# Cutting one weight load of a decode block into 8, 8 and 112 partitions, and joining the loads of x

## The chip, the core and the metric

The kernel runs on one core of a Trainium2 chip. The core has five engines with queues of their own: PE (matrix multiply), DVE (vector), ACT (scalar), POOL, and SP, which here only issues transfers. Sixteen DMA engines carry what SP and ACT issue. The metric is the device time of one execution in microseconds (us), lower is better. Three runs of the kernel before gave a median of 659.67 us (659.04 to 659.94).

## What is computed

Two tokens (batch 2, one position each) go through one attention block with a long cache and one gated feed-forward block:

```python
def ref(x, k_cache, v_cache, wq, wo):          # layernorm(x) comes in
    q = (x @ wq).reshape(B, Sq, Hq, Dh).transpose(0, 2, 1, 3)
    scores = einsum("bhqd,bhkd->bhqk", q, k_cache) * Dh ** -0.5
    o = einsum("bhqk,bhkd->bhqd", softmax(scores), v_cache)
    return o.transpose(0, 2, 1, 3).reshape(B, Sq, Hq * Dh) @ wo

h = x + ref(layernorm(x), k_cache, v_cache, wq, wo)
n = layernorm(h)
gate, up = n @ W_gate, n @ W_up
out = h + ((gate * (gate > 0)) * up) @ W_down
```

B is 2, D is 512, there are 32 heads of Dh = 128 and 8192 cached positions; F of the feed-forward block is 1376. Everything is bf16. Keys and values are 2 x 32 x 8192 x 128 x 2 bytes = 134.2 MB each, so the kernel has to read 268.4 MB of cache and some 12.6 MB of weights, for two rows of output.

## The kernel before

**Tiles.** The cache is walked in steps of four heads (`Step`, lines 130 to 157): 15 full steps, and then the last four heads as two half steps of two heads (`p0`, `p1`). A full key or value tile has 128 partitions of 64 KB, 8.4 MB; a half one has half of that. Three buffers `bufs[0]` to `bufs[2]` (printed as `tile`) hold them in turn. For each step DVE multiplies keys by the query (`products`, L375), folds the products by halves (`scores`, L393, L395); PE does part of the tokens by transposing (L349) and multiplying (L340); ACT takes the exponentials; PE multiplies by the values (`values`, L446).

**Loads.** All large loads are issued by SP in the order of the program (`load_tile`, L165): W_q, the first keys and values, then a key or a value tile whenever a buffer comes free. A load that has to wait holds back all that SP issues after it. The order around the end is: keys of `p0` and `p1`, values of `p0`, the first sixteen heads of W_o (`load_set(0)`, L567 and L571), values of `p1`, the rest of W_o (sets of 8, 4 and 2 heads by `load_set`, then heads 30 and 31 by L589 and L590), W_gate and W_up (L612), W_down (L616, L621). `load_set(k)` puts n heads of W_o into 128 partitions so that each partition gets one contiguous row of n x 1024 bytes: 16 KB for the first set.

**x.** The two rows of x go to two partitions of `xr`, which lies in `bufs[2]` beside W_q. ACT issues five loads for them (L189 to L192), of 256, 256, 256, 128 and 128 elements, each to one partition. PE transposes x (L238), DVE normalises it (`ln_cols`), PE multiplies it by W_q (L252), and when the queries are spread (L259, L267) the second key tile may be loaded over W_q.

**Completion semaphores.** The framework gives the loads, in program order and over SP and ACT together, eight completion semaphores in turn. A load that takes a semaphore has to wait, on its queue, until the load that had it eight places before has landed, unless that is known already. There are 56 transfers in the program. So a transfer more or less ahead of a load changes which older load it waits for.

**The end.** `attend_set(0)` (L635, instructions of L502) uses the first sixteen heads of W_o while the last values are still on their way. After the values of `p1` (L469), the rest of W_o (L502, L509), the second layer norm without its scale (L659 to L677), W_gate and W_up (L686) and W_down (L719), two rows are written out (L736).

Of the kernel before, what the change touches and what calls it, by code (L numbers as in the profile page):

```python
# [13 lines left out]
def _free(t, offset, dims):  # L14

    return bass.AP(tensor=t.tensor, offset=t.offset + offset, ap=[t.ap[0]] + [list(d) for d in dims])


def _dram(t, offset, dims):
    return bass.AP(tensor=t.tensor, offset=t.offset + offset, ap=[list(d) for d in dims])  # L20
# [3 lines left out]
def kernel(  # L24
# [13 lines left out]
    nc = tc.nc  # L38
    P = nc.NUM_PARTITIONS
    B, Sq, D = A_x.shape  # L40
    _, Hkv, Sk, Dh = A_k_cache.shape
# [83 lines left out]
    wo = bufs[0][:, HALF:TILE]  # L125
# [60 lines left out]

    with tc.manual_schedule():

        for b, k, n in ((0, 0, 2), (0, 2, 2), (1, 0, 2), (1, 2, 1), (1, 3, 1)):  # L189
            nc.scalar.dma_start(  # L190
                out=xr[b:b + 1, k * P:(k + n) * P], in_=_dram(A_x, b * D + k * P, [[D, 1], [1, n * P]]),
            )  # L192
# [9 lines left out]
            out=nscale, in_=nscale, compare_op=ALU.not_equal, fill=-SCALE,  # L202
# [5 lines left out]
            out=ident_f, in_=ident_f, compare_op=ALU.not_equal, fill=1.0,  # L208
# [4 lines left out]
            out=sel, in_=sel, compare_op=ALU.not_equal, fill=1.0,  # L213
# [9 lines left out]
            out=pick, in_=pick, compare_op=ALU.not_equal, fill=1.0,  # L223
# [24 lines left out]
        for g0 in range(0, NQ, 4):  # L248
            for n0 in range(NH * g0 * Dh, NH * (g0 + 4) * Dh, 4 * Dh):
                q_ps = ps2.tile([B, 4 * Dh], f32, tag="o")  # L250
                for c in range(KC):
                    nc.tensor.matmul(  # L252
                        out=q_ps, lhsT=xn[:, c, :], rhs=wq_sb[:, c, n0:n0 + 4 * Dh], start=(c == 0), stop=(c == KC - 1),
                    )
                nc.vector.tensor_copy(qrow[:, n0:n0 + 4 * Dh], q_ps)
            for b in range(B):
                r_ps = ps2.tile([P, 4, Dh], f32, tag="tp")
                for j in range(NH):
                    nc.tensor.matmul(  # L259
                        out=r_ps[j * (P // NH):(j + 1) * (P // NH)], lhsT=sel[:, b, 0:P // NH],  # L260
# [5 lines left out]
        for j in range(2):  # L266
            nc.tensor.matmul(  # L267
                out=r_ps[j * (P // 2):(j + 1) * (P // 2)], lhsT=sel[:, B - 1, :],
# [31 lines left out]
        def own_sums(i):  # L300
            b, g0, n = groups[i]
            nc.vector.tensor_tensor(
                out=zc[:, b, g0:g0 + n, :], in0=_free(zs, b * NQ + g0, [[1, n], [0, NH]]),
                in1=_free(own, 0, [[0, n], [1, NH]]), op=ALU.mult,
            )
# [65 lines left out]
        def products(s, t0=0, t1=None):  # L371

            n = (s.nv if t1 is None else t1) - t0
            kv = _free(s.kt, t0 * Dh, [[Dh, n], [1, Dh]])
            nc.vector.tensor_tensor(out=kv, in0=kv, in1=_free(s.qr, 0, [[0, n], [1, Dh]]), op=ALU.mult)  # L375
# [186 lines left out]
        place_own(s)  # L562
        products(p0, 0, p0.na)
        own_sums(Q)
        def load_set(k):
            h0, n, at = SETS[k]
            nc.sync.dma_start(  # L567
                out=wo[:, at * D:(at + n) * D], in_=_dram(A_wo, h0 * Dh * D, [[n * D, P], [1, n * D]]),
            )

        load_set(0)  # L571
        products(p0, p0.na)

        at = [0, 0]
# [12 lines left out]
        for k in range(1, len(SETS)):  # L587
            load_set(k)
        nc.sync.dma_start(out=wo[:, HM * D:(HM + 1) * D], in_=_dram(A_wo, HM * Dh * D, [[D, P], [1, D]]))  # L589
        nc.sync.dma_start(  # L590
            out=wo[:, (HM + 1) * D:Hq * D], in_=_dram(A_wo, (HM + 1) * Dh * D, [[P // 4 * D, 4], [D, P // 4], [1, D]]),
# [19 lines left out]
        for w, src in ((0, B_W_gate), (1, B_W_up)):  # L611
            nc.sync.dma_start(  # L612
                out=wgu[:, w].rearrange("p c f -> p (c f)"), in_=_dram(src, 0, [[KC * F, P], [1, KC * F]]),
            )
        for q0 in range(AGAIN, P, AGAIN):
            nc.sync.dma_start(  # L616
                out=wd_sb[q0:q0 + AGAIN, FC - 1, :], in_=_dram(B_W_down, (F - P + q0) * D, [[D, AGAIN], [1, D]]),
            )
        for f0, n in FSETS[:-1]:
# [10 lines left out]
            out=z2_ps, lhsT=ones, rhs=_free(zc, ((B - 1) * NQ + groups[Q][1]) * NH, [[1, nb]]), start=True, stop=True,  # L630
# [63 lines left out]
        for c in range(KC):  # L694
            nc.tensor.transpose(hT_ps[:, c, :], hb[:, c].rearrange("p k b -> p (k b)"), ident)
        nc.scalar.activation(
            out=hrow.rearrange("q (p c) -> q p c", c=KC), in_=hT_ps.rearrange("q c p -> q p c"), func=ACT.Copy,
# [9 lines left out]
            out=gate, in0=g_ps, scalar=0.0, in1=_free(rvar, 0, [[0, FC], [1, B]]), op0=ALU.max, op1=ALU.mult,  # L707
# [59 lines left out]
```

## Time and profile before

| what | value |
|---|---|
| median of three runs | 659.67 us (659.04 to 659.94) |
| the profiled execution: its own time / its span | 659.39 us / 657.5 us |
| bytes moved, mean rate | 281.37 MB, 428 GB/s |
| busy: DVE, PE, ACT, POOL | 85%, 54%, 19%, 4% |
| mean granted PE clock | 0.76 |

The span runs from the first to the last instruction; the execution's own time is 1.9 us longer. A chain of waits is followed back from the last instruction to what released each step. Beside instructions the trace holds one record for each packet that a DMA engine moved: when it began, how long it took, how many bytes it had and the queue that it came from. It does not name the engine. Here a row of one partition is one packet, and each engine ends a load with a packet of 4 bytes. On one engine a packet begins where the one before it ended, so that the packets of an engine can be followed by their times. Such numbers are called packet records below.

### The profile page before, as it was taken

To read this page: it belongs to the slowest core of one execution; us is meant where nothing else is said; L and a number is where in the kernel's file an instruction comes from. 1 tells how busy PE (TensorE), PEld (TensorE's weight loads), DVE (VectorE), ACT (ScalarE), POOL (GpSimd) and SP (SyncE) were. 2 spreads that over 40 slices of the span, in tenths; PEclk is the share of its full clock that TensorE was granted. 3 is DMA by queue.
4 is the path that set the end of the run, shared out by engine and by line. 5 is a ranking of instruction groups with operands and counts; after the bars stand their busy time and mean duration, and the time that the engine had idled before them with its cause. 6 is when DMAs were issued, how large, how long until landed. Compare 5 with 4: busy or idle time off the path is not lost.

```text
span 657.5 us, 5117 instructions
## 1 busy us (share of the span) xinstructions
PE 352.1 (54%) x2118; PEld 158.9 (24%) x2118; DVE 558.1 (85%) x252; ACT 123.6 (19%) x337; POOL 24.1 (4%) x36
## 2 busy tenths in 40 slices
PE   0730934809175380926539092552918458291997
PEld 0310311304022130312204031220403224030456
DVE  0599697988979799897979989796997969999982
ACT  0230030200203020030301103030210304201870
POOL 3080000000000000000000000000000000000020
PEclk9975775958778596877959687695968869686895
DMA  9999999999999999999999999999999999999997
GB/s 383 447 444 447 387 440 443 447 399 444 439 443 436 419 436 435 439 439 436 423 443 424 439 440 427 447 416 443 439 423 440 423 443 436 423 444 413 425 425 291
DMA packets 6948, 281.37 MB, mean 428 GB/s; under 512 B 809, under 2 KB 1422, under 8 KB 1934
## 3 DMA queue, kind: packets, MB, share of 16 engines
q1 hardware_dynamic: 6916, 281.06, 99.1%
q8 instruction: 16, 0.26, 0.1%
q14 instruction: 6, 0.05, 0.0%
q10 hardware_dynamic: 10, 0.00, 0.0%
HBM read 281.05 MB, written 0.00 MB: 427 GB/s over the span
## 4 chain that ended last, share of the span: by engine, by line
DVE 42%; DMA 37%; PE 18%; ACT 1%; issue 1%; ACTq 0%; SPq 0%; DVEq 0%
DMA tile<-in_A_k_cache_dram 30%; DVE tile L375 19%; DVE tile L393 18%; PE pv_ps L446 16%; DMA tile<-in_A_wo_dram 4%; DVE scol L395 2%; DMA tile<-in_A_x_dram 2%; DMA tile<-in_B_W_down_dram 1%; PE q_ps L252 1%; DVE pgq L420 1%; ACT ecol L415 1%; DVE pm L399 1%; DVE qrep L395 0%; DVE pm L410 0%; DVE hmax L412 0%
## 5 line engine op out<-in xcount | busy, mean ns | idle before, releaser
L446 PE MATMUL pv_ps<-tile,pgq 128*16 128x512 bf16 x960 | 244.3, 421 | 235.8 <-DVE pgq L420 223.2
L375 DVE TENSOR_TENSOR tile<-tile,qrep 128x29696 bf16<-128x29696 bf16 (+3 forms) x16 | 232.4, 14524 | 44.9 <-DMA tile<-in_A_k_cache_dram 44.9
L393 DVE TENSOR_TENSOR tile<-tile 128x14848 bf16<-128x14848 bf16 (+7 forms) x68 | 236.4, 3477 | 2.2
L446 PEld LDWEIGHTS <-pgq 128*16 128x16 bf16 x960 | 91.6, 97 | 378.1 <-DVE pgq L420 234.5
L451 ACT ACTIVATE pv<-pv_ps 16x512 f32<-16x512 f32 (+1 forms) x16 | 9.4, 589 | 243.7 <-PE pv_ps L446 243.6
L350 ACT ACTIVATE tile<-t_ps 128x1024 bf16<-128x1024 bf16 x53 | 52.6, 1022 | 12.6 <-PE t_ps L349 12.1
L415 ACT ACTIVATE ecol<-scol,nmax 128x256 bf16<-128x256 f32 x14 | 7.1, 508 | 196.1 <-DVE nmax L414 196.1
L340 PE MATMUL row_ps<-tile,qz 128*24 128x512 bf16 (+1 forms) x98 | 30.1, 389 | 18.0 <-ACT tile L350 17.9
L349 PE MATMUL t_ps<-ident,tile 128*128 128x128 bf16 x424 | 32.3, 229 | 13.0 <-DMA tile<-in_A_k_cache_dram 13.0
L349 PEld LDWEIGHTS <-tile 128*128 128x128 bf16 x424 | 25.8, 103 | 28.1 <-issue 14.2
L395 DVE TENSOR_REDUCE scol<-tile 128x232 f32<-128x1856 bf16 (+1 forms) x14 | 28.9, 2067 | 0.5
L641 POOL TENSOR_TENSOR tile<-ident 6x2 bf16<-6x2 bf16 x1 | 2.1, 2147 | 583.5 <-ACT tile L381 583.5
L420 DVE TENSOR_TENSOR pgq<-ecol,ownb 128x1024 bf16<-128x1024 bf16 x15 | 10.4, 692 | 10.3 <-ACT ecol L415 10.3
L381 ACT ACTIVATE tile<-tile 128x128 bf16<-128x128 bf16 x60 | 17.6, 293 | 1.9 <-DVE tile L375 1.9
L281 POOL COPY qzp<-qTs 128x4 bf16<-128x4 bf16 x1 | 15.0, 14982 | 26.1 <-DVE qTs L276 26.1
L375 DVE TENSOR_TENSOR tile<-tile,qpair 128x4096 bf16<-128x4096 bf16 (+3 forms) x4 | 15.5, 3883 | 0.0
L340 PEld LDWEIGHTS <-qz 128*24 128x24 bf16 (+1 forms) x98 | 7.9, 92 | 27.6 <-issue 22.7
L239 DVE CAST xc<-x_ps 128x8 f32<-128x8 bf16 x1 | 0.2, 167 | 15.5 <-PE x_ps L238 15.5
L367 ACT ACTIVATE scol<-sc_ps 32x24 f32<-32x24 f32 (+1 forms) x56 | 11.7, 209 | 7.7 <-PE sc_ps L362 7.2
L362 PE MATMUL sc_ps<-ident_f,tile 24*128 24x24 f32 (+2 forms) x68 | 7.2, 220 | 11.1 <-ACT tile L358 11.1
L358 ACT ACTIVATE tile<-row_ps 24x512 f32<-24x512 f32 (+2 forms) x17 | 10.0, 586 | 13.5 <-PE row_ps L340 13.5
L381 ACT ACTIVATION_READ_ACCUMULATOR tile<-tile 128x1 f32 x60 | 11.2, 186 | 0.0
(133 smaller groups left out, 143.8 us busy)
## 6 DMA issues: line engine op xcount, KB each, us to landing
tile<-in_A_k_cache_dram SPq DMA_DIRECT2D x2, 4096.0 KB
tile<-in_A_v_cache_dram SPq DMA_DIRECT2D x2, 4096.0 KB, 19.6
tile<-in_A_wq_dram SPq DMA_DIRECT2D x1, 4096.0 KB, 12.2
tile<-in_A_wo_dram SPq DMA_DIRECT2D x1, 2048.0 KB
tile<-in_B_W_gate_dram SPq DMA_DIRECT2D x1, 1376.0 KB, 22.8
tile<-in_B_W_up_dram SPq DMA_DIRECT2D x1, 1376.0 KB
tile<-in_A_wo_dram SPq DMA_DIRECT2D x1, 1024.0 KB, 23.8
tile<-in_B_W_down_dram SPq DMA_DIRECT2D x1, 640.0 KB
```

The source lines that it names most:

```text
L281: nc.gpsimd.tensor_copy(qzp[:, :, 6:8], qTs[:, B - 1, Hq - NH:Hq].rearrange("p (k j) -> p k j", j=2),)
L340: nc.tensor.matmul(out=row_ps, lhsT=z, rhs=s.kt[:, (nv + c0 + k) * Dh:(nv + c0 + k + 4) * Dh], start=(u == 0), stop=(u == U - 1),)
L349: nc.tensor.transpose(t_ps[:, k, :], s.kt[:, t * Dh:(t + 1) * Dh], ident)
L350: nc.scalar.activation(out=s.kt[:, (nv + c0) * Dh:(nv + c0 + TPC) * Dh], in_=t_ps.rearrange("p t s -> p (t s)"), func=ACT.Copy,)
L367: nc.scalar.activation(out=scols[s.i][r, nv:s.nt].rearrange("p (u t) -> p t u", t=4), in_=sc_ps[r, :, :, j], func=ACT.Copy,)
L375: nc.vector.tensor_tensor(out=kv, in0=kv, in1=_free(s.qr, 0, [[0, n], [1, Dh]]), op=ALU.mult)
L381: nc.scalar.activation(out=kv, in_=kv, func=ACT.Copy, accum_out=scols[s.i][:, t:t + 1])
L393: nc.vector.tensor_tensor(out=lo, in0=lo, in1=hi, op=ALU.add)
L395: nc.vector.tensor_reduce(out=scol[:, s.na:s.nv], in_=_free(s.kt, s.na * Dh, [[Dh, s.nv - s.na], [1, 8]]), axis=AXIS.X, op=ALU.add,)
L415: nc.scalar.activation(out=ecol, in_=scols[s.i], func=ACT.Exp, scale=SCALE, bias=nmax, accum_out=zs[:, s.b, s.g:s.g + 1],)
L420: nc.vector.tensor_tensor(out=s.pg, in0=_free(ecol, 0, [[VG, s.nt // VG], [0, NH], [1, VG]]), in1=_free(ownb, 0, [[0, s.nt // VG], [VG, NH ...
L446: nc.tensor.matmul(out=pv_ps[s.i][r, :], lhsT=s.pg[:, u].rearrange("p j t -> p (j t)"), rhs=s.vt[:, u * VG * Dh:(u + 1) * VG * Dh], start= ...
```

## The change

The first sixteen heads of W_o are loaded by three transfers, of partitions 0 to 7, 8 to 15 and 16 to 127, instead of one. The rows and their bytes stay the same, and the three are issued one after another where the one was. x is loaded by three transfers of 512, 256 and 256 elements instead of five. There are again 56 transfers.

```diff
-        for b, k, n in ((0, 0, 2), (0, 2, 2), (1, 0, 2), (1, 2, 1), (1, 3, 1)):
+        for b, k, n in ((0, 0, 4), (1, 0, 2), (1, 2, 2)):
             nc.scalar.dma_start(
                 out=xr[b:b + 1, k * P:(k + n) * P], in_=_dram(A_x, b * D + k * P, [[D, 1], [1, n * P]]),
             )
...
-        def load_set(k):
+        def load_set(k, cuts=(0, P)):
             h0, n, at = SETS[k]
-            nc.sync.dma_start(
-                out=wo[:, at * D:(at + n) * D], in_=_dram(A_wo, h0 * Dh * D, [[n * D, P], [1, n * D]]),
-            )
-
-        load_set(0)
+            for q0, q1 in zip(cuts, cuts[1:]):
+                nc.sync.dma_start(
+                    out=wo[q0:q1, at * D:(at + n) * D],
+                    in_=_dram(A_wo, (h0 * Dh + q0 * n) * D, [[n * D, q1 - q0], [1, n * D]]),
+                )
+
+        load_set(0, (0, 8, 16, P))
```

The other calls, `load_set(1)` to `load_set(3)`, have no cuts and stay one transfer each.

## Prediction

> **What bounds the kernel now.** I read the page's slices and queues first, then stretches of the span, then the chain of waits, then SP's timeline, and last the packet records.
>
> The slices and the queues of the page (packets, MB, share of 16 engines):
>
> ```profile
> DMA  9999999999999999999999999999999999999997
> q1 hardware_dynamic: 6916, 281.06, 99.1%
> q8 instruction: 16, 0.26, 0.1%
> q10 hardware_dynamic: 10, 0.00, 0.0%
> ```
>
> The DMA engines are busy from the first slice to the last but one. The stretches (busy time of PE, PEld, DVE, ACT, POOL; granted clock, DMA share, GB/s) say the same:
>
> ```profile
> 31.00:330.00 299.00, 148.26 (x756) 63.65 (x755) 266.46 (x85) 46.50 (x97) 14.98 (x1) 0.74 1.00 434
> 330.00:600.00 270.00, 147.26 (x738) 63.13 (x738) 241.59 (x88) 43.41 (x87) 0.00 (x0) 0.76 1.00 433
> 620.00:640.00 20.00, 18.50 (x173) 10.12 (x172) 18.50 (x22) 15.52 (x80) 3.66 (x2) 0.99 0.99 422
> ```
>
> The packet records give the rate of one engine: the 3840 packets of 64 KB take 2418 ns each, almost without exception, so 27.1 GB/s, and sixteen times that is 434. Each of the sixteen carries eight rows of every 128-partition load, one after another, in the order of issue. The kernel ends when the slowest of the sixteen has done its share. DVE's 85% is beside it.
>
> The chain of waits (start, us, what):
>
> ```profile
> 2.11 12.96 DMA tile<-in_A_x_dram
> ...
> 30.96 41.50 DMA tile<-in_A_k_cache_dram
> 72.48 15.64 DVE tile L375
> ...
> 618.99 24.67 DMA tile<-in_A_wo_dram
> ...
> 644.18 9.77 DMA tile<-in_B_W_down_dram
> 653.94 0.04 issue
> 653.99 0.60 PE d_ps L719 x15
> 654.58 0.03 issue
> 654.61 0.33 PE d_ps L719 x4
> ```
>
> x heads it and the last W_down load closes it: PE's last four products start when the last rows land. SP's timeline about the loads in question:
>
> ```profile
> 605.16 0.33 SPq L165 DMA_DIRECT2D tile<-in_A_v_cache_dram  x1
> 605.54 0.42 SPq L567 DMA_DIRECT2D tile<-in_A_wo_dram  x1
> 617.67 0.33 SPq L165 DMA_DIRECT2D tile<-in_A_v_cache_dram  x1
> ...
> 624.84 0.33 SPq L612 DMA_DIRECT2D tile<-in_B_W_gate_dram  x1
> 629.68 0.33 SPq L612 DMA_DIRECT2D tile<-in_B_W_up_dram  x1
> 639.34 4.03 SPq L616 DMA_DIRECT2D tile<-in_B_W_down_dram  x3
> ```
>
> SP runs far ahead: W_o's first set is issued at 605.5 and has landed by 629.7, when W_up, which waits for it, goes out.
>
> **Who is slowest.** Following the packets, the engines finish W_up in three groups: six at 647.8 to 648.0, three at 649.3 to 649.6, seven at 650.7 to 650.9. The spread is made by the sixteen instruction packets of queue q8: each holds up one engine by a pause of about 0.95 us and a next packet of 2890 instead of 2418 ns, 1.4 us in all. They go round eight engines in turn (the engine of 37 us again at 440, that of 95 at 500), so eight get two each by the end (seven of them before W_up ends) and eight none; two of the latter get two 8 KB instruction packets instead, some 0.7 us each. The engine that carries x ends in the first group, as far as its packets can be told from others.
>
> **The change, part by part.**
>
> *x.* On its engine each x load is a data and a 4-byte packet, and between any two of these the queue gives way to one W_q packet of 1213 ns: about 2.45 us a load. The 4-byte packets end at 1.9, 7.6, 10.1, 12.5 and 15.0 us. With three loads the last is the third, 10.1: 4.9 us earlier (bounds: 2.45 if the longer rows cost a turn more, 4.9). From x to normalised x takes 3.4 us (15.20 to 18.56), so 13.6, when W_q's last packet (12.9) has landed; the L252 products move from 18.6 to 13.7 and the second key load from 31.0 to 26.1. What hides it: the first values fill the queue until about 51.6 (first keys landed at 32.2, plus 8 x 2.42), and DVE's first products start at 32.41, 0.2 us after those keys. So 0; the cover is 20 us deep. Two packet pairs fewer on one engine are 0.05 us.
>
> *SP's queue.* Two more issues of 0.43 + 0.05 us at 605.5, 1.0 us. Behind them stands the L165 load of 617.67, which waits for PE: hidden under 11 us.
>
> *Completion semaphores.* The total is 56 again, so from the values of `p1` on each load has the same semaphore as before, but the older users differ. Heads 24 to 27 and 28 to 29 now wait for the key halves of `p0` and `p1` (landed before 618: free), head 30 for the values of `p0` (624.8), head 31, W_gate and W_up for the three pieces. Before, head 30 went out at 619.5 and W_gate waited for those values. All SP work behind head 30 is thus held until 624.8 and then follows the pieces. At that moment the values of `p1` (9.7 us) are still queued, so with pieces up to 5 us late the engines don't run dry: 0. `attend_set(0)` runs at 634.6 and has 4.9 us of room.
>
> *The pieces.* A row is a packet, so a load of 8 partitions occupies eight engines at most, one 16 KB packet each, and 112 partitions are seven packets on each of sixteen. A 16 KB packet takes 613 ns (mean of 128). If both small loads go to the same eight engines, these carry nine packets instead of eight, +0.61 us, and the others seven, -0.61 us. The x loads bear out that a small load is not spread: ten packets for five loads. [...]
>
> *Eight streams into eight partitions.* The trace has no such load. Lower end: each engine keeps its pace, 0.61 us a load; upper end: all eight packets go one after another, 4.9 us. Two rows bound it closer. The 32-partition W_down loads (sixteen streams, two partitions a stream) show packets of 46 ns, as 128-partition loads of the same row do, so two partitions a stream are enough: four streams into eight partitions, two turns, 1.2 us. In the large loads sixteen streams share 128 partitions, eight a stream: one stream, 4.9 us. I take the middle of these by ratio, four partitions a stream, four turns of 0.613: 2.45 us a load. The W_down rows, taken alone, would make it 0.61. [...] By the W_down row the time would be 659.1. Packets of 1 KB may be too short to show it.
>
> *Sum.* The lower eight: 2 x 2.45 + 7 x 0.613 = 9.19 us where eight packets took 4.90: +4.3. The 112-partition load is taken at seven packets' time, its nearest row being the 128-partition one; its upper end is four streams a turn in all seven turns, 17.2 us. How much reaches the end depends on who these eight are: if they hold one of the last group, all 4.3; if all end at 648, 4.3 - 3.1 = 1.2. As x's engine is of the first group, I take them to be the eight that get no 16 KB instruction packets; the latest of those end W_up at 649.6, 1.3 us before the last. So +3.0 us. Behind it W_down follows on the same engines, and PE from the values of `p1` (639.3) to W_up (651.3) has only 0.3 us of idle before W_up, so both move with the slowest engine. On the profiled execution 659.39 + 3.0 = 662.4; the median of the runs shown is 0.28 above it, so 662.7.
>
> **The rivals.**
>
> *No sharing, 0.15.* Each engine keeps its pace (the 46 ns rows speak for it; sixteen engines never pass 434 GB/s together, which leaves room for the opposite). Then the nine packets fall on engines with 1.3 us of slack, and the last group, which sets the end, carries one packet less: -0.61 us, 659.1. It decides as soon as a small load costs under about 1.2 us. This one isn't slower.
>
> *Sharing in the 112 rows too, 0.25.* Seven rows an engine no longer lie as in a 128-partition load. If streams meet two at a time, that load takes 8.6 instead of 4.3 us: 4.3 more, 667.0; on all sixteen engines there is no slack for it. Only the regular packets of the 128-partition loads speak against it.
>
> *The two small loads on different eights, 0.05.* Every engine has eight packets again, and the turns fall apart: 659.7, no change.
>
> *x reaches the end, 0.05.* If the 12.96 us of x at the head of the chain were the true bound, 4.9 us would go: 654.8. The DMA share of 1.00 from 31 us on speaks against it.
>
> **How the numbers follow.** The forecast, 0.50, is 662.7, its own range 660.5 to 664.5 (slack 3.1 to none). The range for 8 in 10 reaches from the no-sharing case, 658.8, to 668.0, just above the 112-row case. This kernel's measurement can tell about 0.2% (1.3 us) from no change. Slower: 0.25 and 0.46 of the forecast's 0.50 = 0.71. Within: 0.15, 0.05 and the forecast's low end 0.04 = 0.24. Faster: 0.05.
>
> **What would show it.** Right: x's last completion at 10.1 us, the second key load issued near 26, and no gain from either at 72; 16 KB packets of the small loads longer than 613 ns, about 2.4 us; W_up's issue, which waits for the 112 rows, near 634 instead of 629.7; the last W_down product about 3 us later. Wrong: those packets at 611 ns (then 659.1), or packets of the 112 rows well above 613 ns (then 667 and more), or an instruction packet that falls on another engine, 1.4 us either way.

## The result, and the profile after

| | before | changed |
|---|---|---|
| median of four runs | 659.58 us (659.04 to 659.94) | 667.40 us (666.47 to 668.18) |
| the profiled execution, its own time / its span | 659.39 / 657.5 us | 668.18 / 666.4 us |
| mean rate of the span | 428 GB/s | 422 GB/s |

The changed kernel is slower: ratio 1.0119, 95% interval 1.0104 to 1.0134, or 7.8 us. The forecast was +3.0 us. The time lies near the upper end of the range, at the rival "Sharing in the 112 rows too" (667.0).

The slices and queues of the changed kernel's page (rows and queues as before, with the rate of each slice):

```profile
DMA  9999999999999999999999999999999999999996
GB/s 378 441 438 441 441 438 425 401 441 438 441 433 438 437 430 433 429 429 442 429 441 426 437 438 429 441 434 429 441 430 429 433 438 437 430 414 437 290 369 252
q1 hardware_dynamic: 6932, 281.06, 98.8%
q8 instruction: 16, 0.26, 0.1%
q10 hardware_dynamic: 6, 0.00, 0.0%
```

The busy row shows nothing: every slice but the last is a 9. The rate shows it: one slice (the 38th, 616 to 633 us) has 290 GB/s where its neighbour has 437. The stretches of the changed kernel say so more sharply (columns: busy time of PE, PEld, DVE, ACT, POOL; granted clock, DMA share, GB/s):

```profile
31.00:330.00 299.00, 146.31 (x740) 62.74 (x740) 265.95 (x83) 45.95 (x94) 0.00 (x0) 0.74 1.00 434
330.00:600.00 270.00, 147.23 (x738) 62.97 (x738) 241.72 (x88) 43.41 (x87) 0.00 (x0) 0.75 1.00 433
620.00:640.00 20.00, 15.76 (x111) 7.26 (x110) 17.15 (x14) 14.79 (x77) 3.50 (x2) 1.00 1.01 275
```

Up to 600 us nothing has changed. Between 620 and 640 the DMA engines are as busy as ever (1.01) and move 275 GB/s instead of 422: their packets take longer. In 20 us, 147 GB/s less is 2.9 MB, which at 434 GB/s takes 6.8 us to make good. That is most of the loss in one line.

The chain of waits of the changed kernel (start, us, what):

```profile
1.51 8.62 DMA tile<-in_A_x_dram
...
26.93 45.70 DMA tile<-in_A_k_cache_dram
...
72.75 15.64 DVE tile L375
...
619.28 33.23 DMA tile<-in_A_wo_dram
...
653.02 9.79 DMA tile<-in_B_W_down_dram
662.81 0.04 issue
662.85 0.60 PE d_ps L721 x16
...
663.48 0.33 PE d_ps L721 x4
```

x lands at 10.1 instead of 15.1 us and the second key load goes out 4.0 us earlier; yet the product of these keys begins at 72.75 instead of 72.48. The W_o piece of the chain is one of the loads of the rest of W_o, which queue behind the first set and the values of `p1`; it has grown from 24.67 to 33.23 us, and the last product begins at 663.48 instead of 654.61, 8.9 us later.

SP's timeline of the changed kernel (start, us, line, what is issued):

```profile
605.26 0.33 SPq L165 DMA_DIRECT2D tile<-in_A_v_cache_dram  x1
605.64 1.05 SPq L568 DMA_DIRECT2D tile<-in_A_wo_dram  x3
617.94 0.36 SPq L165 DMA_DIRECT2D tile<-in_A_v_cache_dram  x1
...
630.09 0.33 SPq L614 DMA_DIRECT2D tile<-in_B_W_gate_dram  x1
638.89 0.33 SPq L614 DMA_DIRECT2D tile<-in_B_W_up_dram  x1
648.29 3.92 SPq L618 DMA_DIRECT2D tile<-in_B_W_down_dram  x3
```

W_up, which waits for the 112-partition piece, goes out at 638.89; before, it went at 629.68, and the forecast was about 634. Two places on PE show who waits for the late bytes (PE's timeline, in brackets the idle time before and what ended it; the kernel before first, then the changed one):

```profile
634.56 2.29 PE L502 MATMUL att_ps<-orow,tile 128*128 128x2 bf16 x64
...
639.46 1.84 PE L469 MATMUL o_ps<-pgp,tile 128*128 128x2 bf16 x64 [0.67 <-ACT pgp L433]
```

```profile
638.96 2.27 PE L502 MATMUL att_ps<-orow,tile 128*128 128x2 bf16 x64 [4.06 <-DMA tile<-in_A_wo_dram]
...
648.28 1.87 PE L469 MATMUL o_ps<-pgp,tile 128*128 128x2 bf16 x64 [4.89 <-DMA tile<-in_A_v_cache_dram]
```

`attend_set(0)` (L502) had to wait for no load before; it now waits for W_o. The values of `p1`, of 32 KB a partition (L469), are late as well, although nothing about them was changed.

The packet records (after 600 us, all sixteen engines; excess is what the packets took beyond the pace of 611 or 1213 ns, divided by sixteen):

| packets | before: mean, longest, excess | changed: mean, longest, excess |
|---|---|---|
| 16 KB, W_o's first set (128) | 613, 855 ns, 0.02 us | 1167, 1634 ns, 4.45 us |
| 32 KB, keys and values of the half steps (some 420) | 1214, 1762 ns, 0.03 us | 1318, 3156 ns, 2.80 us |

Nearly all 128 packets of W_o's first set are slow, not the sixteen of the two small loads alone: three kept to 611 ns. The first set is on its way from 621.5 to 637.9 us (before: 621.6 to 629.5). Nearly all of the excess in the 32 KB packets falls on the 256 of the values. Together the two kinds hold 7.25 us an engine. The profiled execution is 8.8 us longer than the one before, and is the slowest of the four; the remaining 1.6 us I have not assigned (pauses between packets and engines that end later than the mean are not told apart).

### The profile page after: what moved, and what is told of

Same layout as the page of the kernel before. It is cut to its first block, busy times and chain, and to the rows that moved or that the text cites. A ratio compares the mean times of both kernels' runs of the same rounds, so it can differ in the third digit from the quotient of the medians.

```text
span 666.4 us, 5116 instructions
## 1 busy us (share of the span) xinstructions
PE 353.0 (53%) x2118; PEld 159.7 (24%) x2118; DVE 558.2 (84%) x252; ACT 123.6 (19%) x337; POOL 9.1 (1%) x36
## 3 DMA queue, kind: packets, MB, share of 16 engines
q1 hardware_dynamic: 6932, 281.06, 98.8%
## 4 chain that ended last, share of the span: by engine, by line
DVE 42%; DMA 38%; PE 18%; ACT 1%; issue 1%; SPq 0%; ACTq 0%; DVEq 0%
DMA tile<-in_A_k_cache_dram 30%; DVE tile L375 19%; DVE tile L393 18%; PE pv_ps L446 16%; DMA tile<-in_A_wo_dram 5%; DVE scol L395 2%; DMA tile<-in_B_W_down_dram 1%; PE q_ps L252 1%; DMA tile<-in_A_x_dram 1%; DVE pgq L420 1%; ACT ecol L415 1%; DVE pm L399 1%; DVE qrep L395 0%; DVE pm L410 0%; DVE hmax L412 0%
## 5 line engine op out<-in xcount | busy, mean ns | idle before, releaser
L362 PEld LDWEIGHTS sc_ps<-ident_f,tile 24*128 24x128 f32 (+2 forms) x68 | 5.6, 141 | 19.8 <-ACT tile L358 19.8
L252 PE MATMUL q_ps<-tile,xn 128*2 128x512 bf16 x32 | 9.8, 473 | 1.0 <-DVE xn L185 1.0
```

The lines of the kernel that those rows point to most:

```text
L252: nc.tensor.matmul(out=q_ps, lhsT=xn[:, c, :], rhs=wq_sb[:, c, n0:n0 + 4 * Dh], start=(c == 0), stop=(c == KC - 1),)
L362: nc.tensor.transpose(sc_ps[:, t].rearrange("p u j -> p (u j)"), rows[:, t * P:(t + 1) * P], ident_f[0:nh * U, 0:nh * U],)
```

## The experiments

In each comparison both kernels ran on the same chip. The edits are against the kernel before, unless it is said otherwise. Below, a stream is what one engine writes, and a way is what several of the 128 partitions would share, if streams into them slow each other; both are words for a theory that the runs test.

**x alone.**

```diff
-        for b, k, n in ((0, 0, 2), (0, 2, 2), (1, 0, 2), (1, 2, 1), (1, 3, 1)):
+        for b, k, n in ((0, 0, 4), (1, 0, 2), (1, 2, 2)):
```

> Only x comes by three loads; the first sixteen heads of W_o come by one load of 128 partitions as before. Theory A (everything comes from the W_o pieces, whose streams share the way into neighbouring partitions): x lands near 10 us instead of 15, the second key load goes out near 26 instead of 31, and the time stays within 0.7 us of before, 659.0 to 660.3. Rival B (the joined x loads, or the shifted completion semaphores, hold something up): 663 or more. 54 transfers instead of 56, so from the end on the semaphores stand two places away from both kernels; A expects nothing from that.

Measured 659.67 us against 659.27, ratio 1.0005 (0.9996 to 1.0014): no difference. The chain of waits of this kernel:

```profile
1.51 8.69 DMA tile<-in_A_x_dram
...
27.38 44.93 DMA tile<-in_A_k_cache_dram
...
72.43 15.63 DVE tile L375
```

The second keys are issued 3.6 us earlier than before and stay under way that much longer, to the same 72.4.

**The three cuts alone.** `load_set` as in the change, `load_set(0, (0, 8, 16, P))`, x by five loads.

> Only the cut of W_o into 8, 8 and 112 partitions; x by five loads as before. Theory A: the whole loss is here, 666.5 to 668.2, and the 16 KB packets take about 1.15 us instead of 0.61. Rival B (x or the semaphores): under 663.

Measured 667.81 us against 659.27, ratio 1.0132 (1.0115 to 1.0149). The stretch about W_o:

```profile
620.00:640.00 20.00, 17.29 (x145) 9.43 (x144) 16.97 (x15) 14.28 (x73) 3.99 (x2) 0.96 1.01 285
```

The whole loss is here. Its W_o packets take 1174 ns; excess 4.51 us in them and 2.47 us in the values' packets.

**Three loads without a cut across the partitions.** x by three loads, and the same number of loads and the same semaphores as in the change, but each load of W_o covers all 128 partitions, with 8, 4 and 4 KB of each row (the new lines alone).

```diff
+            for c0, c1 in zip(cuts, cuts[1:]):
+                nc.sync.dma_start(
+                    out=wo[:, (at + c0) * D:(at + c1) * D],
+                    in_=_dram(A_wo, (h0 * Dh + c0) * D, [[n * D, P], [1, (c1 - c0) * D]]),
+                )
...
+        load_set(0, (0, 8, 12, 16))
```

> x by three loads, and the first sixteen heads of W_o by three loads, as in the change, but cut along the row: each of the three goes to all 128 partitions, with rows of 8, 4 and 4 KB. Number of transfers and completion semaphores are those of the change. Theory A (streams share the way into neighbouring partitions): every engine keeps its own way, packets at the pace of the 8 KB and 4 KB rows before (309 and 159 ns), no loss, 658.5 to 660.5. Rival E (three loads instead of one, or the semaphore order, cost the time): 663 to 668.

Measured 659.47 us against 659.33, ratio 1.0003 (0.9994 to 1.0013).

```profile
620.00:640.00 20.00, 18.00 (x179) 10.03 (x178) 18.30 (x22) 14.94 (x76) 4.00 (x2) 0.95 0.99 419
```

So neither the number of loads nor the shifted semaphores cost anything. The loss comes from which partitions a load covers.

**Two loads of 64 neighbouring partitions.** `load_set(0, (0, 64, P))`. The page counts 6932 packets on q1, 16 more than before (6916), one of 4 bytes from each engine for the load more: all sixteen take part, and by the count each has four rows of a load.

> x as before; the first sixteen heads of W_o by two loads of 64 partitions each, so that all sixteen engines carry four rows of each and every engine has the eight packets it had. Theory A (streams share the way into neighbouring partitions): the sixteen streams go into half of the partitions at a time; packets of about 1.2 us, W_o takes 4.9 us longer, 663 to 666. Rival C (the uneven shares of the engines, nine packets against seven, or a row count that isn't a power of two, cost the time): packets of 0.61 us, 659 to 660.

Measured 667.02 us against 659.27, ratio 1.0114 (1.0099 to 1.0130), above both expectations; packets of 1184 ns.

```profile
620.00:640.00 20.00, 17.02 (x145) 8.66 (x144) 16.69 (x14) 14.51 (x76) 3.33 (x2) 1.00 1.01 278
```

Uneven shares are not the cause, and neither is a row count that is no power of two. What the theory had left out is the slowing of the values' packets, 2.62 us here.

**Loads by themselves.** Only loads of 16 KB rows, each after the one before, without any of the rest of the kernel.

> Only loads; all computation of the reference is left out and the output is the first rows of x. One after another, each waiting for the one before, rows of 16 KB into: 128 partitions; 0 to 7; 8 to 15; 0, 4, ... 28; 0, 16, ... 112; 0 to 7 and then 0, 4, ... 28 with source rows 2 MB apart; 16 to 127; 32 to 127; 0 to 63; 0 to 31; 0, 8, ... 120; 0 to 15; 0 to 3; all twice. [...] Rival D (source rows that lie close together in memory): far source rows are fast, close ones slow, whatever the partitions. Rival C (uneven or odd row counts): 112 and 96 slow, 8, 16, 32 and 64 at 0.61.

One execution, 150.5 us. Two rounds each:

| partitions | packets, mean ns | first packet of this load to first of the next, us |
|---|---|---|
| 0 to 127 | 706, 723 | 8.06, 7.83 |
| 0 to 63 | 1172, 1179 | 7.07, 7.11 |
| 0 to 31 | 1067, 1091 | 4.95, 5.04 |
| 16 to 127 | 967, 927 | 9.49, 9.06 |
| 32 to 127 | 1102, 1067 | 9.63, 9.58 |
| 0 to 7 | 1007, 1057 | 4.13, 3.95 |
| 0 to 7, source rows far apart | 1105, 1069 | 4.56, 4.51 |
| 8 to 15 | 1282, 1312 | 4.95, 4.87 |
| 0, 4, ..., 28 | 996, 950 | 2.99, 2.98 |
| 0, 4, ..., 28, source rows far apart | 955, 919 | 2.77, 2.72 |
| 0, 16, ..., 112 | 947, 974 | 3.04, 3.07 |
| 0, 8, ..., 120 (16 rows) | 937, 930 | 3.16, 3.13 |
| 0 to 15 | 1540, 1202 | 4.94, 4.09 |
| 0 to 3 (4 rows) | 826, 1045 | 3.92, the last load |

No load here has packets of 0.61 us: they take 0.7 us in the loads of 128 partitions and about 0.95 in those of every fourth, so the packets do not separate loads that are quick in the kernel from slow ones. The times to the next load do: eight neighbouring partitions take 4.0 to 5.0 us, every fourth 2.7 to 3.0, wherever the source rows lie. For loads by themselves the destination decides, not the source. And 64 neighbours take 5.0 us from first to last packet, 128 partitions with twice the bytes 6.4. Every sixteenth and every eighth partition take hardly longer than every fourth (3.0 to 3.2 us); the last run below bears on the former.

**Extra loads of eight neighbours or of every fourth partition.** The kernel before with four more loads, into a part of W_o that is loaded over later; bytes, rows and the 32 partitions are the same in both. Near: `q0, step = 8 * k, 1`. Apart: `q0, step = k, 4`.

```diff
         load_set(0)
+        for k in range(4):
+            q0, step = 8 * k, 1
+            nc.sync.dma_start(
+                out=wo[q0:q0 + 7 * step + 1:step, 16 * D:Hq * D],
+                in_=_dram(A_wo, q0 * 16 * D, [[step * 16 * D, 8], [1, 16 * D]]),
+            )
```

> The kernel before with four more loads behind the first sixteen heads of W_o, of 8 partitions and 16 KB rows each, into a part of the buffer that is loaded anew later: partitions 0 to 7, 8 to 15, 16 to 23, 24 to 31. Eight engines carry four packets more, 2.45 us at 0.61 us a packet. Theory A: eight streams meet in eight neighbouring partitions, packets of 1.2 us or more, and the time is 662 to 668. Without sharing: packets of 0.61 and 659 to 662.

Near: 665.37 us against 659.33, ratio 1.0092 (1.0077 to 1.0107).

```profile
620.00:640.00 20.00, 17.79 (x151) 9.41 (x149) 18.27 (x22) 15.34 (x79) 3.39 (x2) 0.99 1.01 360
```

> The same as the run with neighbouring partitions, the same bytes into the same 32 partitions by four loads of eight, but each takes every fourth partition: 0, 4, ... 28, then 1, 5, ... 29, and so on. [...] If eight streams into few partitions are slow wherever these lie, or any load of eight partitions is: packets of 1.2 us or more, the same time as with neighbours, 662 to 668.

Apart: 661.79 us against 659.33, ratio 1.0038 (1.0024 to 1.0053).

```profile
620.00:640.00 20.00, 17.76 (x147) 9.90 (x145) 17.61 (x20) 14.84 (x75) 3.99 (x2) 0.93 0.99 423
```

Apart costs 2.46 us (by the interval 1.6 to 3.5), where four packets of 0.611 are 2.44, and 159 of its 160 packets of 16 KB take about 611 ns. So the eight engines that take small loads show no slack: the packets more reach the end. Near costs 3.6 us more for the same bytes to the same partitions. Of its 160 packets of 16 KB 66 are slow, 1.03 us in the mean, under the 1.2 expected and far from 2.45; as only 32 are extra ones, the first set's are among them. Values' packets take up to 2487 ns.

The rest of W_o goes where the extra loads go, so SP holds it back until these have landed: it is issued at 631.8 us (apart) and 636.0 (near) instead of 618.1. That does not explain the difference: from 620 to 650 us the DMA share is 1.00 in both, at 421 and 375 GB/s.

**Who has the slack.** The kernel before, with an 8-partition load of 64 bytes a row behind each key or value load, so that one can see in the records which engines carry small loads.

```diff
+    tag = consts.tile([P, 32], bf16)
...
+        nc.sync.dma_start(out=tag[0:29:4, :], in_=_dram(A_wo, 0, [[D, 8], [1, 32]]))
```

> The kernel before with a tiny load (8 partitions, 64 bytes each) behind every key and value load, so that the packet records show which engines belong to the eight that carry a load of 8 partitions. The prediction assumed that these eight get none of the 16 KB instruction packets. Theory A1 (as assumed): all sixteen of those packets fall on engines without the small ones. Rival A2: they fall on both kinds, so the eight include late engines and have no slack. The time itself, about 660 to 664, is of no interest.

One execution, 660.03 us. Of the 16 KB instruction packets, those at 37, 95, 156, 206, 352 and 395 us fall on engines without the small packet, those at 245 and 305 us on engines with it. The rotation repeats after eight, so these two come round again at 622 and 639 us, and two of the eight small-load engines belong to the last group. This agrees with the run before: no slack.

**One load of 112 partitions, without the small ones.** The kernel before with one extra load of partitions 16 to 127, `wo[16:P, 16 * D:Hq * D]`.

> The kernel before with one more load behind the first sixteen heads of W_o: partitions 16 to 127, rows of 16 KB, into a part of the buffer that is loaded anew later. It adds seven packets to each engine, 4.3 us at 0.61. No small loads. If the 112 partitions are slow by themselves (their rows no longer lie on the engines so that each has a way of its own): packets of 0.9 to 1.2 us, and 666 to 671 in all. If the small loads of the change were what slowed everything: packets of 0.61, 662.5 to 664.5.

Measured 670.20 us against 659.23, ratio 1.0176 (1.0159 to 1.0193): 11.0 us for seven packets an engine that take 4.3 us at their own pace.

```profile
620.00:640.00 20.00, 17.45 (x150) 9.23 (x147) 18.29 (x22) 15.00 (x76) 3.75 (x2) 0.97 1.02 295
```

Of 240 packets of 16 KB, 101 keep to 0.6 us, all of them in the first 6 us, when the first set is under way, and some 130 take 1.0 to 1.5. The excess is 4.7 us an engine in them and 1.9 in the values' packets. The 112-partition piece is slow without any small load.

**Four loads of 32 neighbouring partitions.** `load_set(0, (0, 32, 64, 96, P))`.

> The first sixteen heads of W_o by four loads of 32 partitions; x by five loads. [...] If the pace goes with the number of partitions: twice as slow again, packets of 2.4 us, 675 to 680.

Measured 667.45 us against 659.23, ratio 1.0123 (1.0108 to 1.0138), packets of 1174 ns: the same as with loads of 64. Were only the nearness of partitions at work, half as many partitions for sixteen streams would have been worse.

**Two loads of 64, even partitions and odd ones.**

```diff
-        load_set(0)
+        for q0 in range(2):
+            nc.sync.dma_start(
+                out=wo[q0:P:2, 0:16 * D], in_=_dram(A_wo, q0 * 16 * D, [[2 * 16 * D, P // 2], [1, 16 * D]]),
+            )
```

> The first sixteen heads of W_o by two loads of 64 partitions like the run cut at 64, but the even partitions first and then the odd ones; x by five loads. [...] If half of the partitions is half the pace whichever half it is: 1.18 us a packet again, 667.

Measured 659.44 us against 659.23, ratio 1.0003 (0.9993 to 1.0012).

```profile
620.00:640.00 20.00, 18.89 (x191) 10.46 (x190) 18.28 (x22) 15.47 (x79) 3.27 (x2) 1.00 0.99 422
```

Nearly all packets take 611 ns; only two of the 128 were slow. So half of the partitions is not half the pace whichever half it is. How the rows are dealt out to the engines was not measured. The same 64 rows a load cost 7.8 us as neighbours and nothing as every second partition.

**The extra loads again, of every sixteenth partition.** As above with `q0, step = k, 16`.

> The kernel before with the same four extra loads of eight 16 KB rows, now of every sixteenth partition each (0, 16, ..., 112, then 1, 17, ... and so on). They go, like the others, into the part of W_o that is loaded over later. Two theories of what shares a way. Neighbours alone: no two partitions of a load are nearer than sixteen, so its streams don't meet; as with every fourth partition, four packets at 0.611 us on the engines that take them, 659.3 + 2.46 = 661.8 us, 16 KB packets at 611 ns. [...] The probe, where such a load alone took no longer than one of every fourth partition, speaks for the first, but there every packet took about 1 us in any case.

Measured 666.55 us against 659.19, ratio 1.0112 (1.0095 to 1.0129).

```profile
620.00:640.00 20.00, 16.88 (x144) 8.92 (x143) 16.75 (x15) 13.82 (x71) 3.89 (x2) 0.96 1.01 337
```

It is worse than eight neighbours (665.37), though no two partitions of a load are nearer than sixteen. This speaks against "neighbours alone": partitions far apart seem to share a way too. One rival stays. The rows of these loads also lie 256 KB apart in the source (64 KB with every fourth partition, 16 KB with neighbours), and no run has that distance with other partitions in the kernel; in the probe the rows of this load lay side by side.

**What the runs settle together.** Which partitions a load covers decides: the first set with rows of 16 KB and 16 KB apart in the source is quick as one load and slow in loads of 64 or 32 neighbours. Number of loads, semaphores and x were varied and cost nothing, and extra loads of every fourth partition cost no more than their packets' own pace. In the probe, source rows 2 MB apart changed the time to the next load by at most 0.6 us. What all this fits is that a load is quick when its streams go to different ways, and slow when two or more are sent to one. That is inferred from times; which partitions share a way was not measured, and no record names an engine.

## Why the prediction was wrong in size

*x, SP's queue, the semaphores: right.* x's completions came at 1.9, 7.6 and 10.0 us (forecast 10.1). The second key load went out at 26.9 instead of 26.1, since the first W_q products took longer, 6.14 us. Neither reached the end, as x alone (1.0005) and the cuts along the row (1.0003) show.

*That streams into the same partitions slow each other: right*, and with it the sign. Where the sum failed, term by term:

- **The 112-partition piece "taken at seven packets' time".** This is the main error. All of W_o's first set ran at 1167 ns a packet, so seven take 8.2 instead of 4.3 us. The row that I took as nearest, the 128-partition load, was not near: its packets keep to 613 ns, and a block of 112, 64 or 32 neighbours does not inherit that. The rival had the sharing of two streams at a time, and nearly the packet time (1.23 us). That its 667.0 came so close to 667.4 is partly luck: it too has the dear small pieces and the slack, and nothing for the values.
- **The small pieces at 2.45 us each.** Too dear: no W_o packet of the first set took more than 1.63 us, and the slow packets in the run with four extra loads of eight neighbours took 1.03 us in the mean. Four streams a turn were not seen. Engines that reach their packets at different moments would explain it; that was not tested.
- **The slack of 1.3 us.** There is none. I took the small-load engines to be those without 16 KB instruction packets, because x's engine was; two of the eight get them, and the extra loads of every fourth partition cost 2.46 us in full.
- **Nothing for the packets of other loads.** The values on both sides of W_o lost 2.8 us an engine, up to 3156 ns for a packet of 1213. The sum had no such term: I had priced a piece by its own packets only.

In the order of the sum: 4.45 us from W_o's packets and 2.8 us from the values' where I had +3.0. The "No sharing" rival rested on W_down packets of 46 ns; those are of 1 KB, perhaps too short to show how streams meet, as the forecast suspected; that was not tested. Its remark that the engines never pass 434 GB/s together holds for long stretches only: single slices of the page before read up to 447. "The two small loads on different eights" falls with the 112-partition run, since the loss needs no small loads. No run shows the sum's "lower eight", one set of engines under both small loads; what the records show is that 124 of the 128 packets of W_o's first set took over 1.0 us, and that the four extra loads of every fourth partition cost 2.46 us, as four packets on one engine would. Of the signs to look for, x's were met, W_up's issue came at 638.9 instead of 634, and "packets of the 112 rows well above 613 ns (then 667 and more)" was the one that came.

No kernel of this study is faster than the one before; the best are equal to it.

## What to carry to other kernels

In a stage that the DMA engines bound, cut a load along its rows or into every second partition, not into blocks of neighbours: here the first two cost nothing (1.0003 both) and the last 7.8 us on 2.1 MB. Spanning all 128 partitions is not enough: four small loads of every sixteenth cost 7.4 us. Price a partial load by where its rows go, and add the packets of other loads that it meets. Read the rate beside the busy share, since a slow packet counts as busy: the share was 1.01 at 275 GB/s.

## What was unexpected

- A load slows others that have nothing to do with it: 2.5 to 2.8 us an engine in the values' packets in all three kinds of cut (8/8/112, 64/64, four of 32).
- 64 partitions can be as good as 128 or half as fast, by their step alone: 611 or 1184 ns a packet.
- Every sixteenth partition took no longer than every fourth when loaded alone (3.04 and 2.99 us to the next load), yet within the kernel the first cost 7.4 us and the second 2.46. A load measured by itself did not show what it costs among others; that its source rows lay side by side in the one and 256 KB apart in the other may have a part in it.
